# Two modulation vectors held per feature instead of broadcast, with dummy matmuls at launch, the first K in halves, and loads gated by step

## The chip, the cores and the metric

The kernel runs on one core of one Trainium2 chip. The metric is the device time of one execution in microseconds (us); lower is better.

## The reference, cut to what matters

```python
mod = (silu(c) @ w_mod).reshape(1, 6, 1, 640)        # c: (1, 640), w_mod: (640, 3840)
sa, ca, ga, sb, cb, gb = the six vectors of mod

h = layernorm(x) * (1 + ca) + sa                     # x: (2048, 640)
x = x + ga * attention(h, k_cache, v_cache)          # 32 heads of 128, K and V given: 2048 keys
h = layernorm(x) * (1 + cb) + sb
x = x + gb * mixer_and_mlp(h)                        # w1, w2, then w3 (640 x 1728), w4 (1728 x 640)
```

All tensors are bf16. Only `ca` and `sa`, the two vectors of the first line with `h`, are touched by the arithmetic of this change. Everything else in it is about when things are loaded.

## The kernel before

**The build-time schedule.** The program is written as a list of operations on tiles. When the kernel is built, a list scheduler with its own rough cost model puts each engine's operations into a fixed order. On the chip every engine goes through that order and waits on semaphores. Whatever changes a dependence can therefore change the whole order.

```python
    def op(self, eng, fn, dur, reads=(), writes=(), prio=0.0, ..., dep=(), tset=None):
        ...                                   # (cut) read-after-write and write-after-read from tiles
        for d in dep:
            o.deps[d] = True
```

**The stream.** There are 4 chunks (`ch`) of 512 query rows and 32 heads (`h`), so 128 "steps" of some 10 us each. A step loads one head's K (transposed by the DMA), its part of wq and its V, makes Q with five matmuls, and then has eight rounds of two score matmuls, one exp of 128x1024 on ScalarE and eight PV matmuls. The mixer and MLP of chunk `ch` are worked off inside the steps of chunk `ch+1`. All DMA is issued by one engine, SP, in one order.

```python
    def step(ch, h):
        s = ch * H + h
        ...                                   # (cut)
        dma("SP", lambda e: e.dma_start_transpose(k.ap.unsqueeze(1), A_k_cache[0, h]), 560, (), (k,), lp, dur=2600)
        dma("SP", ... w ...)                  # wq of this head, 160 KB
        dma("SP", ... v ...)                  # V of this head, 512 KB
        for kk in range(KT):                  # Q, L462
            P.op("PE", lambda e, kk=kk: e.matmul(m.ap, w[:, kk, :], hT_t[ch % 2][:, kk, :], ...),
                 MM(QC), (w,) + tuple(hT[ch % 2]), (m,), s - 2.0 + 0.17 * kk, accum=True, ...)
        ...                                   # (cut) copy of Q, L465; scores L474, exp L477, PV L487
```

**The modulation vectors.** Each of the six vectors is made on all 128 partitions at once: `s_bc` holds silu(c) repeated 128 times, so ten 128x320 matmuls leave the vector in every row.

```python
    def mod_part(p, stage, prio, dep=()):
        ...                                   # (cut) one load of 800 KB of w_mod
        for hf in range(2):
            ...
                for k in range(KT):           # L340
                    ins = e.matmul(m[:, 0:HD], s_bc[:, k, :], wv[:, k, sl], start=(k == 0), stop=(k == KT - 1))
            ...                               # (cut) ScalarE (L344) or VectorE (L347) copies it out
    mod_part(CA, 0, -98.9)
    mod_part(SA, 1, -98.5)
```

**The first normalisation.** Four row tiles of 128x640 per chunk, each with two VectorE passes that take the vectors as second inputs, then a transposition: by TensorE and a ScalarE copy in chunk 0, by the DMA later. The intermediate `w` is one of three fp32 scratch tiles.

```python
    tmp = ring("tmp", 3, [128, D], F32)

    def get_tmp():
        n_tmp[0] += 1
        return tmp[n_tmp[0] % 3]

    def modulated(src, src_t, mvt, rst, pc, pb, dst, dst_t, prio):
        w = get_tmp()
        P.op("DVE", ... scalar_tensor_tensor(out=w.ap, in0=src, scalar=mvt[:, 0:1], in1=mod_t[pc][:], ...)   # L388
        P.op("DVE", ... scalar_tensor_tensor(out=dst, in0=w.ap, scalar=rst.ap, in1=mod_t[pb][:], ...)        # L391

    def ln1(ch, i, prio):
        j = ch * 4 + i
        x = first_x[j] if j < 4 else load_x(j, prio - 3)
        mvt, rst = ln(x.ap, (x,), prio)
        h = hA[j % 3]
        modulated(x.ap, x, mvt, rst, CA, SA, h.ap, h, prio)
        ...                                   # (cut) transposition into hT
```

**The other loads.** `load_w4` loads all of w4 three times, once per chunk whose MLP is interleaved. `tail_front` loads w1 and w2 once more for the tail, after the stream, into buffers that have come free; nothing but those buffers holds the ten loads back.

```python
    def load_w4(pr):
        for wt, f0, f1 in ((WA, 0, 5), (WA2, 5, 10), (WA3, 10, NF - 1)):
            dma("SP", ... w4 rows f0*128 to f1*128 ...)
        dma("SP", ... the last 64 rows ..., tuple(WA3), pr + 3.5)

        # in tail_front, L751
        for src, dst in ((B_w1, w1p), (B_w2, w2p)):
            for kk in range(KT):
                dma("SP", ..., 160, (), (dst[kk][1],), base - 3)
```

## Time and profile before

| | before |
|---|---|
| time, median of 3 runs | 1452.18 us (1451.65 to 1453.45) |
| span of the profiled run | 1449.9 us |
| first exp of the stream starts | 26.19 us |
| start of the first exp to start of the last | 1321.85 us |
| from the start of the last exp to the end | 101.83 us |

The page of the profile of before, the engines' busy time, the moved bytes, and the shares of the chain that ended last:

```profile
PE 1400.2 (97%) x13129; PEld 934.4 (64%) x13129; DVE 561.3 (39%) x1325; ACT 1099.1 (76%) x1291; POOL 62.3 (4%) x50
...
DMA packets 745769, 228.37 MB, mean 158 GB/s; under 512 B 708320, under 2 KB 744992, under 8 KB 745632
...
PE 90%; ACT 3%; DMA 2%; issue 2%; POOL 1%; DVE 1%; SPq 0%; POOLq 0%
```

TensorE (PE) is busy for 97% of the span and makes up 90% of the chain. So in the stream, work taken from VectorE is worth nothing by itself; what can be won is time in which TensorE has no work or runs at half clock. Only at launch does VectorE stand in the chain.

The launch, from the chain of waits of before (start in us, length in us, what it was):

```profile
1.81 5.01 DMA f_WA<-in_w_mod_dram
...
6.87 2.86 PE f_M L340 x10
...
10.22 0.88 DVE f_tmp L388
...
13.74 1.58 DVE f_hA L391 x2
...
21.99 3.73 PE f_M L462 x9
25.73 0.45 PE f_S L474 x2
26.19 1.03 ACT f_PT L477
```

One load of w_mod, the matmuls of the broadcast, a copy on ScalarE, and then from 10.2 to 20.5 us mostly VectorE work, with passes of 0.88 us, before Q can start at 21.99 us. The nine Q matmuls take 0.41 us each; in the stream two of them take 0.43 us together. The windows view of before (stretch, its length, busy time of PE, PEld, DVE, ACT and POOL with counts, granted TensorE clock, DMA share, GB/s) shows why:

```profile
15.00:20.00 5.00, 1.46 (x11) 0.90 (x10) 4.31 (x9) 2.59 (x7) 0.00 (x0) 0.51 1.14 230
20.00:25.00 5.00, 3.72 (x13) 1.53 (x14) 1.09 (x2) 0.69 (x1) 0.00 (x0) 0.50 0.73 229
```

The granted clock is half. The Trainium skill ("TensorE: Matmul & The Clock Gate", Part 1, "What's actually happening") says that the clock is half until TensorE has been busy for a window of about 3.4 us; this trace agrees as far as the halving goes.

The stream loses time in a few places. In the timeline of the DMA queue (SP) of before, an entry's length is the time that its issue held the queue:

```profile
104.69 1.63 SPq L751 DMA_DIRECT2D f_s_bc<-in_B_w_dram  x1
106.37 2.56 SPq L457 DMA_TRANSPOSE f_KTs<-in_A_k_cache_dram  x1
...
934.63 4.44 SPq L751 DMA_DIRECT2D f_mod<-in_B_w_dram  x3
939.11 2.76 SPq L457 DMA_TRANSPOSE f_KTs<-in_A_k_cache_dram  x1
```

The timeline of ScalarE in the same stretches (in brackets: how long it sat idle before the group, and what released it):

```profile
109.16 6.52 ACT L477 ACTIVATE f_PT<-f_S 128x1024 bf16<-128x1024 f32 x7 [3.01 <-PE f_S L474]
...
946.39 7.73 ACT L477 ACTIVATE f_PT<-f_S 128x1024 bf16<-128x1024 f32 x8 [4.04 <-PE f_S L474]
```

Both times a load of tail weights stands in the queue ahead of a K, and after it exp has no scores for 3 to 4 us. At the second the K landed at 945.47 us and its first scores ran at 945.71. What such a shortage costs TensorE stands in its timeline:

```profile
947.47 0.61 PE L474 MATMUL f_S<-f_QT,f_KTs 128*128 128x512 bf16 x2 [0.68 <-ACT f_PT L477]
948.38 0.60 PE L474 MATMUL f_S<-f_QT,f_KTs 128*128 128x512 bf16 x2 [0.31 <-ACT f_PT L477]
```

With its PV matmuls used up, TensorE makes one pair of scores per exp: a pair every 0.91 us. The view shows a gap of 0.31 us.

A second measure is used in this document, called **lost TensorE time**: the elapsed time of a stretch less the work issued in it, where each matmul counts as its columns at 2.4 GHz plus 2.5 ns. It is an estimate. The two constants are those of the Trainium skill ("TensorE: Matmul & The Clock Gate", "Wait — 56ns, not 53.3ns?"), and this trace agrees nearly: most 512-column matmuls of the stream start 215 ns after the one before and most 129-column ones 56 ns, but some of the latter take 60 and the last one before a pair of scores 70, so eight take 0.46 us in the chain and not 0.45. Counting goes by the weight loads, since some matmul records are missing from some traces.

A caution on the zero of this measure. A recount from the two constants alone comes out higher than the tables below, by some 1.85% of the work in every stretch. With that share taken off, the recount meets every cell within 0.5 us. So the tables' zero is the pace of a stretch that nothing disturbs. Differences between kernels hold to about half a microsecond; a level depends on where the zero is put.

### The profile page before, as it was taken

The numbers are of one execution on the slowest core, as the hardware profiler recorded it, in microseconds if no ns is written. First come the engines' busy times: TensorE is split into PE (matmuls) and PEld (weight loads), VectorE is DVE, ScalarE is ACT, GpSimd is POOL, SyncE is SP. The second block draws the span as 40 slices with busy tenths as digits, with TensorE's granted clock in tenths as the row PEclk, the third lists the DMA queues.
The fourth block names the chain that finished last, engine by engine and source line by source line (L and its number), as shares of the span: only waits on it lengthen the run. The fifth ranks groups of instructions, "written<-read, shape, count | busy, mean of one in ns | idle before, by whom it ended". The sixth has DMA issues, their size and how long they took to land.

```text
span 1449.9 us, 30338 instructions
## 1 busy us (share of the span) xinstructions
PE 1400.2 (97%) x13129; PEld 934.4 (64%) x13129; DVE 561.3 (39%) x1325; ACT 1099.1 (76%) x1291; POOL 62.3 (4%) x50
## 2 busy tenths in 40 slices
PE   5999999999999999999999999999999999999987
PEld 3565666676666666666666666666666656666654
DVE  5332222334742226222844224422464322233662
ACT  4868888887888685788888785678888869887441
POOL 1000000000000000000000000000002100002450
PEclk8999999999999999999999999999999999999999
DMA  7997899999989577998989755999897959886000
GB/s 187 206 221 140 159 173 180 176 202 191 181 160 189 114 144 160 203 176 169 181 172 178 153 115 116 213 199 169 165 177 167 178 99 159 166 167 143 26 6 24
DMA packets 745769, 228.37 MB, mean 158 GB/s; under 512 B 708320, under 2 KB 744992, under 8 KB 745632
## 3 DMA queue, kind: packets, MB, share of 16 engines
q1 hardware_dynamic: 745632, 226.39, 79.1%
q8 instruction: 105, 1.72, 0.5%
q14 instruction: 32, 0.26, 0.1%
HBM read 134.61 MB, written 2.62 MB: 95 GB/s over the span
## 4 chain that ended last, share of the span: by engine, by line
PE 90%; ACT 3%; DMA 2%; issue 2%; POOL 1%; DVE 1%; SPq 0%; POOLq 0%
PE f_O L487 31%; PE f_S L474 29%; PE f_M L462 9%; PE f_M L522 9%; PE f_M L686 3%; ACT f_PT L477 2%; PE f_M L709 2%; PE f_S L903 1%; DMA f_KTs<-in_A_k_cache_dram 1%; PE f_M L887 1%; PE f_M L646 1%; PE f_M L665 1%; PE f_S L860 1%; PE f_M L340 1%; ACT f_us L847 0%
## 5 line engine op out<-in xcount | busy, mean ns | idle before, releaser
L477 ACT ACTIVATE f_PT<-f_S 128x1024 bf16<-128x1024 f32 x1024 | 999.2, 1024 | 224.3 <-PE f_O L487 110.0
L487 PEld LDWEIGHTS f_O<-f_V,f_PT 128*128 128x128 bf16 x8192 | 547.8, 98 | 226.2 <-DVE f_On L498 21.7
L487 PE MATMUL f_O<-f_V,f_PT 128*128 128x129 bf16 x8192 | 641.2, 220 | 1.5 <-DVE f_On L498 0.9
L474 PE MATMUL f_S<-f_QT,f_KTs 128*128 128x512 bf16 x2048 | 602.2, 379 | 16.3 <-ACT f_PT L477 13.3
L465 DVE CAST f_QT<-f_M 128x512 bf16<-128x512 f32 x128 | 88.4, 691 | 476.0 <-PE f_M L462 475.9
L462 PE MATMUL f_M<-f_hT,f_wq 128*128 128x512 bf16 x640 | 226.0, 381 | 0.8 <-ACT f_hT L411 0.8
L474 PEld LDWEIGHTS f_S<-f_QT,f_KTs 128*128 128x128 bf16 x2048 | 165.1, 97 | 82.5 <-ACT f_PT L477 41.0
L522 PE MATMUL f_M<-f_wo,f_OT 128*128 128x320 bf16 x992 | 173.3, 299 | 0.2
L530 DVE TENSOR_TENSOR f_yacc<-f_M,f_yacc 128x320 f32<-128x320 f32 x216 | 105.7, 489 | 146.9 <-PE f_M L522 146.4
L522 PEld LDWEIGHTS f_M<-f_wo,f_OT 128*128 128x128 bf16 x992 | 89.9, 97 | 56.2 <-DVE f_yacc L530 6.0
L498 DVE TENSOR_TENSOR f_On<-f_O,f_rl 128x256 bf16<-128x256 f32 x256 | 107.9, 421 | 6.6
L496 DVE RECIPROCAL f_rl<-f_O 128x2 f32<-128x2 f32 x256 | 43.3, 169 | 159.2 <-PE f_O L487 154.4
L462 PEld LDWEIGHTS f_M<-f_hT,f_wq 128*128 128x128 bf16 x640 | 62.1, 97 | 45.4 <-issue 1.9
L686 PE MATMUL f_M<-f_nT,f_WB 128*128 128x512 bf16 (+3 forms) x210 | 44.1, 362 | 0.0
L690 ACT ACTIVATE f_gT<-f_M 128x512 bf16<-128x512 f32 (+3 forms) x42 | 23.6, 561 | 26.6 <-PE f_M L686 26.6
L709 PE MATMUL f_M<-f_WA,f_gT 128*128 128x320 bf16 x196 | 37.0, 299 | 0.0
L573 POOL COPY f_us<-f_us 128x660 bf16<-128x660 bf16 x3 | 2.2, 736 | 770.2 <-PE f_M L665 770.2
L686 PEld LDWEIGHTS f_M<-f_nT,f_WB 128*128 128x128 bf16 (+1 forms) x210 | 19.6, 98 | 19.6 <-ACT f_gT L690 2.2
L891 ACT ACTIVATE f_gT<-f_M 128x384 bf16<-128x384 f32 (+4 forms) x22 | 11.2, 510 | 18.7 <-PE f_M L887 18.7
L709 PEld LDWEIGHTS f_M<-f_WA,f_gT 128*128 128x128 bf16 x196 | 17.9, 97 | 10.1 <-issue 2.7
L650 ACT ACTIVATE f_us<-f_M 32x512 bf16<-32x512 f32 (+3 forms) x27 | 16.0, 594 | 9.4 <-PE f_M L646 9.0
L903 PE MATMUL f_S<-f_WA,f_gT 128*128 128x320 bf16 (+1 forms) x140 | 21.2, 300 | 0.6 <-ACT f_gT L891 0.6
(126 smaller groups left out, 572.1 us busy)
## 6 DMA issues: line engine op xcount, KB each, us to landing
f_V<-in_A_v_cache_dram SPq DMA_DIRECT2D x128, 512.0 KB, 5.1
f_wq<-in_A_wq_dram SPq DMA_DIRECT2D x128, 160.0 KB, 2.9
f_wo<-in_A_wo_dram SPq DMA_DIRECT2D x32, 640.0 KB, 5.1
f_xin<-in_A_x_dram SPq DMA_DIRECT2D x32, 160.0 KB, 3.5
f_WA<-in_B_w_dram SPq DMA_DIRECT2D x30, 160.0 KB, 3.5
f_WA<-in_B_w_dram SPq DMA_DIRECT2D x6, 800.0 KB, 6.4
out_dram<-f_ob SPq DMA_DIRECT2D x16, 160.0 KB, 1.8
f_WA<-in_w_mod_dram SPq DMA_DIRECT2D x3, 800.0 KB, 5.0
```

Of the source, the lines that this page charges most:

```text
L462: P.op("PE", lambda e, kk=kk: e.matmul(m.ap, w[:, kk, :], hT_t[ch % 2][:, kk, :], start=(kk == 0), stop=(kk == KT - 1)), MM(QC), (w,) + tu ...
L465: P.op("DVE", lambda e: e.tensor_copy(q.ap, m.ap), dve(QC, True), (m,), (q,), s - 4)
L474: ins = e.matmul(sp[:, r * QC:(r + 1) * QC], k[:, kt * 128:(kt + 1) * 128], q.ap, start=True, stop=True)
L477: last_exp[s, j] = P.op("ACT", lambda e, sp=sp, pt=pt: e.activation(pt.ap.rearrange("p k q -> p (k q)"), sp.ap, ACT.Exp, scale=SCALE), 104 ...
L487: ins = e.matmul(o[b][:, u * 129:u * 129 + 129], pt[:, r, qt * 128:(qt + 1) * 128], v[:, kt, 0:129], start=(kt == 0 and u == 0), stop=(kt ...
L496: P.op("DVE", lambda e, ov=ov, i0=i0: e.reciprocal(rl_t[:, i0:i0 + 2].unsqueeze(2), ov[:, 0:258].rearrange("p (u d) -> p u d", u=2)[:, :, ...
L498: P.op("DVE", lambda e, ov=ov, i0=i0, b=b: e.tensor_tensor(out=On_t[gs][:, 2 * b:2 * b + 2, hh, :], in0=ov[:, 0:258].rearrange("p (u d) -> ...
L522: ins = e.matmul(m[:, 0:HD], OT_t[gs][:, qt, hh, :], w[:, hh, sl], start=(hh == 0), stop=(hh == HG - 1))
L530: P.op("DVE", lambda e, m=m, qt=qt, sl=sl: e.tensor_tensor(out=y_t[:, qt, sl], in0=m[:, 0:HD], in1=y_t[:, qt, sl], op=ALU.add), dve(HD, Tr ...
L686: ins = e.matmul(m[0:fs[f], 0:n], w3v[:, kk, f * 128:f * 128 + fs[f]], nT_t[:, kk, r0:r1], start=(kk == 0), stop=(kk == KT - 1))
L709: ins = e.matmul(m[:, 0:HD], gT_t[0:fs[f], f, i * 128:(i + 1) * 128], w4v[0:fs[f], f, sl], start=(f == 0), stop=(f == NF - 1))
L903: ins = e.matmul(m[:, hf * 512:hf * 512 + HD], gT_t[0:fs[f], f, i * 128:(i + 1) * 128], w4v[0:fs[f], f, hf * HD:(hf + 1) * HD], start=(f = ...
```

## The change

The intent as the diff shows it, in five parts.

1. **Per feature.** `ca` and `sa` are no longer broadcast. 50 one-column matmuls leave them as columns, one value per partition (`hm`). The normalisation becomes one VectorE pass without them; after the transposition, where features lie on partitions, five scales of 128x512 apply them. The fp32 scratch tile is not needed any more. The launch gets a new order with it: the x rows are loaded before w_mod, the normalisation goes earlier, and the copy into `s_bc` goes later.
2. **Dummy matmuls.** 144 matmuls of 128x128 at launch, on the identity matrix, to raise the clock.
3. **First K in halves**, so that the first scores need only the first half.
4. **Gates.** The x rows of chunks 1 to 3, and the ten tail weights, may be issued only after the first exp of a given step. The last part of w4 (560 KB) gets loaded once instead of three times.
5. **Own buffer for four tail weights**, as the fp32 vectors whose space they used are gone.

```diff
     def op(self, ...):
-        for d in dep:
-            o.deps[d] = True
+        o.late = dep                    # resolved in schedule(), so that a gate may name a later operation
...
+    for i in range(36):
+        m = Tile(pool="M")
+        def warm(e, m=m):
+            for r in range(4):
+                ins = e.matmul(m[:, r * 128:(r + 1) * 128], ident_t[:], ident_t[:], start=True, stop=True)
+            return ins
+        P.op("PE", warm, 4 * 56, (ident,), (m,), -10)
...
+    for kk in range(KT):
+        def mm_mod(e, kk=kk):
+            for n in range(2 * KT):
+                ins = e.matmul(m_mod[:, n:n + 1], wmv[:, kk, n * 128:(n + 1) * 128], c_f[:, kk:kk + 1], ...)
+            return ins
+        P.op("PE", mm_mod, 2 * KT * 60, (WA[kk], c_f), (m_mod,), -98, accum=True)
...
-    mod_part(CA, 0, -98.9)
-    mod_part(SA, 1, -98.5)
...
     def ln1(ch, i, prio):
-        x = first_x[j] if j < 4 else load_x(j, prio - 3)
+        x = first_x[j] if j < 4 else load_x(j, prio - 3, (lambda: last_exp[ch * H - 22 + 2 * i, 0],))
...
-        modulated(x.ap, x, mvt, rst, CA, SA, h.ap, h, prio)
+        P.op("DVE", lambda e: e.tensor_scalar(out=h.ap, in0=x.ap, scalar1=mvt[:, 0:1], scalar2=rst.ap,
+             op0=ALU.subtract, op1=ALU.mult), 400, (x, mvt, rst), (h,), prio)
...
+    def scale_h(ch, prio):
+        for k in range(KT):
+            v = hT_t[ch % 2][:, k, :]
+            ...                         # k == 2 of chunk 0 on ScalarE
+            P.op("DVE", ... tensor_scalar(out=v, in0=v, scalar1=hm[:, KT + k:KT + k + 1], scalar2=hm[:, k:k + 1],
+                 op0=ALU.mult, op1=ALU.add), 340, tuple(hN[ch % 2]) + (hm,), (hT[ch % 2][k],), prio)
...
     def step(ch, h):
-        dma("SP", lambda e: e.dma_start_transpose(k.ap.unsqueeze(1), A_k_cache[0, h]), 560, (), (k,), lp, dur=2600)
+        for i, (r0, r1) in enumerate(((0, SK // 2), (SK // 2, SK)) if s == 0 else ((0, SK),)):
+            dma("SP", lambda e, r0=r0, r1=r1: e.dma_start_transpose(k[:, r0:r1].unsqueeze(1), ...), ...)
...
-                 MM(QC), (w,) + tuple(hT[ch % 2]), (m,), s - 2.0 + 0.17 * kk, accum=True,
+                 MM(QC), (w, hT[ch % 2][kk]), (m,), s - 2.0 + 0.17 * kk, accum=True,
...
+            dma("SP", ... w4v[:, 10:NF - 1, :] ..., tuple(WA3), base - 16, (last_exp[base - 16, 0],))
+            dma("SP", ... w4v[0:FL, NF - 1, :] ..., tuple(WA3), base - 15, (last_exp[base - 15, 0],))
...
-        for wt, f0, f1 in ((WA, 0, 5), (WA2, 5, 10), (WA3, 10, NF - 1)):
+        for wt, f0, f1 in ((WA, 0, 5), (WA2, 5, 10)):
...
-                dma("SP", ..., 160, (), (dst[kk][1],), base - 3)
+                sl = base - 19 + (n * KT + kk) // 2
+                dma("SP", ..., 160, (), (dst[kk][1],), base - 3, (last_exp[sl, 0],))
```

More of the change, by code (lines that the diff above doesn't have):

```diff
@@ L85, in schedule @@
             o.order = {d() if callable(d) else d for d in o.order}
+            for d in o.late:
+                o.deps[d() if callable(d) else d] = True
             pre = set(o.deps) | o.order
@@ L276, in fast_path @@
     mod = [[T(None), T(None)] for _ in range(6)]
-    mod_t = [sb("mod%d" % i, [128, D], F32) for i in range(6)]
+    mod_t = [None, None] + [sb("mod%d" % i, [128, D], F32) for i in range(2, 6)]
+    hm = T(sb("hm", [128, 2 * KT], F32)[:])
+    wt_t = sb("wt", [128, 4 * D], BF16)
     rl_t = sb("rl", [128, 4 * NC * H], F32)
@@ L302, in back_to_exp @@
         return (o,)
-    c_sb, c_e, c_f = small("c_sb", KT, BF16), small("c_e", KT), small("c_f", KT)
+    c_sb, c_e, c_f = small("c_sb", KT, BF16), small("c_e", KT), small("c_f", KT, BF16)
     s_bc = T(sb("s_bc", [128, KT, 128], BF16)[:])
@@ L313, in fast_path, with load_x @@
     n_x = [0]
-    def load_x(j, prio):
+    def load_x(j, prio, dep=()):
         t = xin[n_x[0] % 4]
         n_x[0] += 1
-        dma("SP", lambda e: e.dma_start(t.ap, x2d[j * 128:(j + 1) * 128, :]), 160, (), (t,), prio)
+        dma("SP", lambda e: e.dma_start(t.ap, x2d[j * 128:(j + 1) * 128, :]), 160, (), (t,), prio, dep)
         return t
-    first_x = [load_x(j, -99 + 0.4 * j) for j in range(4)]
+    first_x = [load_x(j, -99.8 + 0.1 * j) for j in range(4)]
+    wmv = WA_t[:, 0:KT * 2 * D].rearrange("p (k n) -> p k n", k=KT)
+    for kk in range(KT):
+        dma("SP", lambda e, kk=kk: e.dma_start(wmv[:, kk, :], w_mod[kk * 128:(kk + 1) * 128, 0:2 * D]), 320, (), (WA[kk],), -99 + 0.1 * kk)
+    for i in range(36):
[5 more added lines that the diff above has]
+        P.op("PE", warm, 4 * 56, (ident,), (m,), -10)
     P.op("ACT", lambda e: e.activation(c_e.ap, c_sb.ap, ACT.Exp, scale=-1.0), 300, (c_sb,), (c_e,), -90)
@@ L326, in fast_path @@
     P.op("DVE", lambda e: e.tensor_mul(out=c_f.ap, in0=c_e.ap, in1=c_sb.ap), 100, (c_e, c_sb), (c_f,), -90)
-    P.op("DVE", lambda e: e.tensor_copy(s_bc.ap, c_f.ap.unsqueeze(2).to_broadcast([128, KT, 128])), 700, (c_f,), (s_bc,), -90)
+    P.op("DVE", lambda e: e.tensor_copy(s_bc.ap, c_f.ap.unsqueeze(2).to_broadcast([128, KT, 128])), 700, (c_f,), (s_bc,), 0)
+    m_mod = Tile(pool="O1")
+    for kk in range(KT):
+        def mm_mod(e, kk=kk):
+            for n in range(2 * KT):
+                ins = e.matmul(m_mod[:, n:n + 1], wmv[:, kk, n * 128:(n + 1) * 128], c_f[:, kk:kk + 1], start=(kk == 0 and n == 0),
+                               stop=(kk == KT - 1), skip_group_check=True)
+            return ins
+        P.op("PE", mm_mod, 2 * KT * 60, (WA[kk], c_f), (m_mod,), -98, accum=True)
+    P.op("DVE", lambda e: e.tensor_copy(hm[:, 0:KT], m_mod[:, 0:KT]), 170, (m_mod,), (hm,), -98)
+    P.op("DVE", lambda e: e.tensor_scalar(out=hm[:, KT:2 * KT], in0=m_mod[:, KT:2 * KT], scalar1=1.0, scalar2=None, op0=ALU.add),
+         170, (m_mod,), (hm,), -98)
     def mod_part(p, stage, prio, dep=()):
@@ L376, in fast_path @@
     hT_t = [sb("hT%d" % i, [128, KT, QC], BF16) for i in range(2)]
-    hT = [[T(None) for _ in range(4)] for _ in range(2)]
+    hN = [[T(None) for _ in range(4)] for _ in range(2)]
+    hT = [[T(None) for _ in range(KT)] for _ in range(2)]
     hA = ring("hA", 3, [128, D], BF16)
@@ L396, in ln1 @@
         j = ch * 4 + i
-        x = first_x[j] if j < 4 else load_x(j, prio - 3)
+        x = first_x[j] if j < 4 else load_x(j, prio - 3, (lambda: last_exp[ch * H - 22 + 2 * i, 0],))
         mvt, rst = ln(x.ap, (x,), prio)
         h = hA[j % 3]
-        modulated(x.ap, x, mvt, rst, CA, SA, h.ap, h, prio)
-        dst, dt_ = hT_t[ch % 2][:, :, i * 128:(i + 1) * 128], hT[ch % 2][i]
+        P.op("DVE", lambda e: e.tensor_scalar(out=h.ap, in0=x.ap, scalar1=mvt[:, 0:1], scalar2=rst.ap, op0=ALU.subtract, op1=ALU.mult),
+             400, (x, mvt, rst), (h,), prio)
+        dst, dt_ = hT_t[ch % 2][:, :, i * 128:(i + 1) * 128], hN[ch % 2][i]
         if ch == 0:
@@ L413, in ln1 @@
         else:
-            dma("SP", lambda e: e.dma_start_transpose(dst, h.ap), 160, (h,), (dt_,), prio, dur=1250)
+            dma("SP", lambda e: e.dma_start_transpose(dst, h.ap), 160, (h,), (dt_,), prio,
+                tuple(o for t in hT[ch % 2] for o in t.readers[-1:]), dur=1250)
+    def scale_h(ch, prio):
+        for k in range(KT):
+            v = hT_t[ch % 2][:, k, :]
+            if ch == 0 and k == 2:
+                P.op("ACT", lambda e, k=k, v=v: e.activation(v, v, ACT.Identity, scale=hm[:, KT + k:KT + k + 1], bias=hm[:, k:k + 1]),
+                     act(QC), tuple(hN[ch % 2]) + (hm,), (hT[ch % 2][k],), prio)
+                continue
+            P.op("DVE", lambda e, k=k, v=v: e.tensor_scalar(out=v, in0=v, scalar1=hm[:, KT + k:KT + k + 1], scalar2=hm[:, k:k + 1],
+                                                            op0=ALU.mult, op1=ALU.add),
+                 340, tuple(hN[ch % 2]) + (hm,), (hT[ch % 2][k],), prio)
     for i in range(4):
-        ln1(0, i, -80 + i)
+        ln1(0, i, -97 + 0.1 * i)
+    scale_h(0, -96)
     wq = ring("wq", 2, [128, KT, 128], BF16)
     KTs = ring("KTs", 2, [128, SK], BF16)
+    KTh = [[T(None), T(None)] for _ in range(2)]
     V = ring("V", 2, [128, NKT, 130], BF16)
@@ L456, in step @@
         lp = s - 2.5 if s > 1 else -97 + s
-        dma("SP", lambda e: e.dma_start_transpose(k.ap.unsqueeze(1), A_k_cache[0, h]), 560, (), (k,), lp, dur=2600)
+        kh = KTh[s % 2]
+        for i, (r0, r1) in enumerate(((0, SK // 2), (SK // 2, SK)) if s == 0 else ((0, SK),)):
+            dma("SP", lambda e, r0=r0, r1=r1: e.dma_start_transpose(k[:, r0:r1].unsqueeze(1), A_k_cache[0, h, r0:r1, :]), 560 * (r1 - r0) / SK, (),
+                (kh[i],) if s == 0 else tuple(kh), lp, dur=2600 * (r1 - r0) / SK)
         dma("SP", lambda e: e.dma_start(w.ap, A_wq[:, h * 128:(h + 1) * 128].rearrange("(k p) d -> p k d", p=128)), 160, (), (w,), lp - 0.5)
@@ L475, in smm @@
                 return ins
-            last_s[s] = P.op("PE", smm, 2 * MM(QC), (k, q), (sp,), s + j / 8 - 1.0)
+            last_s[s] = P.op("PE", smm, 2 * MM(QC), (kh[j // 4], q), (sp,), s + j / 8 - 1.0)
             last_exp[s, j] = P.op("ACT", lambda e, sp=sp, pt=pt: e.activation(
@@ L559, in load_w123 @@
         if ch == 0:
+            dma("SP", lambda e: e.dma_start(w4v[:, 10:NF - 1, :], B_w4[1280:(NF - 1) * 128, :].rearrange("(f p) n -> p f n", p=128)), 480, (),
+                tuple(WA3), base - 16, (last_exp[base - 16, 0],))
+            dma("SP", lambda e: e.dma_start(w4v[0:FL, NF - 1, :], B_w4[(NF - 1) * 128:FF, :]), 80, (), tuple(WA3), base - 15, (last_exp[base - 15, 0],))
             for kk in range(KT):
@@ L565, in load_w4 @@
     def load_w4(pr):
-        for wt, f0, f1 in ((WA, 0, 5), (WA2, 5, 10), (WA3, 10, NF - 1)):
+        for wt, f0, f1 in ((WA, 0, 5), (WA2, 5, 10)):
             dma("SP", lambda e, f0=f0, f1=f1: e.dma_start(w4v[:, f0:f1, :], B_w4[f0 * 128:f1 * 128, :].rearrange("(f p) n -> p f n", p=128)),
                 160 * (f1 - f0), (), tuple(wt), pr + f0 * 0.3)
-        dma("SP", lambda e: e.dma_start(w4v[0:FL, NF - 1, :], B_w4[(NF - 1) * 128:FF, :]), 80, (), tuple(WA3), pr + 3.5)
     def carry(ch, pr):
@@ L588, in held @@
         fv = [hT_t[0][:].rearrange("p k q -> p (k q)").bitcast(F32)[:, i * D:(i + 1) * D] for i in range(2)]
-        fvt = [like(hT[0]) for _ in range(2)]
+        fvt = [like(hT[0] + hN[0]) for _ in range(2)]
         for t in tl:
@@ L741, in tail_front @@
         carry(ch, base - 2)
-        ca, sa = [mod_t[p][:].bitcast(BF16) for p in (CA, SA)]
-        mca, msa = [[like(mod[p]) for _ in range(2)] for p in (CA, SA)]
+        wt = [(wt_t[:, i * D:(i + 1) * D], T(None)) for i in range(4)]
         on = On_t[0][:].rearrange("p a b c -> p (a b c)")
         ont = [like(On[0]) for _ in range(2)]
-        w1p = [(hA[i].ap, hA[i]) for i in range(3)] + [(ca[:, i * D:(i + 1) * D], mca[i]) for i in range(2)]
-        w2p = [(sa[:, i * D:(i + 1) * D], msa[i]) for i in range(2)] + [(s_bc.ap.rearrange("p k q -> p (k q)"), s_bc)] + \
+        w1p = [(hA[i].ap, hA[i]) for i in range(3)] + wt[0:2]
+        w2p = wt[2:4] + [(s_bc.ap.rearrange("p k q -> p (k q)"), s_bc)] + \
               [(on[:, i * D:(i + 1) * D], ont[i]) for i in range(2)]
-        for src, dst in ((B_w1, w1p), (B_w2, w2p)):
+        for n, (src, dst) in enumerate(((B_w1, w1p), (B_w2, w2p))):
             for kk in range(KT):
-                dma("SP", lambda e, src=src, dst=dst, kk=kk: e.dma_start(dst[kk][0], src[kk * 128:(kk + 1) * 128, :]), 160, (), (dst[kk][1],), base - 3)
+                sl = base - 19 + (n * KT + kk) // 2
+                dma("SP", lambda e, src=src, dst=dst, kk=kk: e.dma_start(dst[kk][0], src[kk * 128:(kk + 1) * 128, :]), 160, (), (dst[kk][1],),
+                    base - 3, (last_exp[sl, 0],))
         return w1p, w2p
@@ L762, in tail @@
         slots = [KTs[0].ap, KTs[1].ap] + [V[i].ap.rearrange("p k d -> p (k d)") for i in range(2)]
-        own = [KTs[0], KTs[1], V[0], V[1]]
+        own = [like(KTh[0]), like(KTh[1]), V[0], V[1]]
         xt = {t0: (x1[t0 % NX], xb[t0 % NX])}
@@ L952, in fast_path @@
                     ln1(ch + 1, i, ch * H + 10 + 2 * i)
+                scale_h(ch + 1, ch * H + 19)
         if ch < NC - 1:
```

## The prediction

> **What bounds the kernel.** TensorE: the page has PE busy 1400.2 of 1449.9 us (ScalarE 1099, VectorE 561), and PE work is 90% of the chain that ended last. Gaps between PE instructions in the trace sum to about 41 us: 14.5 in the first 22 us, about 15 in the attention stream, about 10 in the tail after 1340 us. The change can touch only the first two, so the gain stays below 2%.
>
> **Launch.** The chain of waits before: w_mod load (1.81 to 6.82 us), 128x320 matmuls, ScalarE eviction, then VectorE with eight two-input modulation passes of 0.88 us, BN halves and copies of 0.48 us, PE transposes; Q matmuls at 21.99, first scores at 25.35, first exp at 26.19 us. The Q matmuls ran cold, 0.43 us apart against 0.22 later. The Trainium skill ("TensorE: Matmul & The Clock Gate", Part 1) says the clock is halved until about 3.4 us of activity; the windows view agrees (granted 0.5 from 15 to 25 us).
>
> After: two broadcast vectors become 50 one-column matmuls and two ten-column copies (about 0.2 us each); the eight passes become four one-input bf16 passes (0.61 us from f32 in this trace; estimate 0.4) plus five 128x512 scales (estimate 0.35, one on ScalarE), and Q starts as each scale lands. Summing: last normalised tile near 12.5 us, its transposed copy near 14.5, Q near 15.5, first exp near 18. The 1.6 MB of w_mod should land by 10 to 11 us (before: by 9.6). Halving the first K matters little. The 144 dummy matmuls end near 10 us, about when the first transposes are ready; they may not hold the clock up through the thin stretch to 15 us. Gain: about 8 us, 5 to 9.
>
> **Stream.** The DMA queue issues in order, so a load that waits blocks the next K. Timeline before: a tail weight load into s_bc held it 1.63 us at 104.7, scores ran out, exp sat 3.0 us and PE lost 2.0; three tail loads held it 4.44 us at 934.6, exp sat 4.0 and 2.8 us and PE lost 3.9; at 587.7 a K issue took 6.7 us behind a burst with x and a w4 part, PE lost 1.9; chunk-1 x and w4 loads at 17 to 42 us precede 3 us of PE idle at 60 to 92. The change gates tail loads and x by exp step, and loads the last w4 part once, not three times (1.1 MB less). Gaps at 209 and 1078 us (late K behind transposes, 1.3 and 1.1 us) remain. I expect 6 us back of these 10.8. VectorE work saved later is off the path; the tail is unchanged.
>
> **Predicted: 1438 us**, 1431 to 1446 in 8 of 10. Faster by over 2%: 0.04; within 2%: 0.95; slower: 0.01.
>
> **What would show it.** First exp at 17 to 20 us (timeline); Q matmuls 0.22 us apart; no queue wait of microseconds on tail weight loads, no exp gap of 3 us near 100 and 930 us; PE gaps about 27 us in all; VectorE busy some 15 us lower; 1 MB less moved.
>
> **What would make it wrong.** w_mod landing after 11 us, or dummy matmuls holding back the transposes, loses half the launch gain. A cold clock at Q costs 1 to 2 us. The rescheduled stream could open new late-K gaps of 1 to 3 us that cancel the 6; or more K delays than the PE gaps show could vanish, down to 1431.

## More of the kernel before

A state is known only for repeated runs. Every run told of here was in the fast state, so all comparisons are of fast runs with fast runs.

(Before the first clock record of a trace, which lies at 11.64 us in before, the view reads 1.00 whatever the clock was: ten 320-column matmuls took 2.86 us at 6.87 us, and 1.36 us in the stream.)

## The result, and the profile after

| | before | after |
|---|---|---|
| time, median | 1452.65 us (4 runs) | 1431.85 us (4 runs, 1430.38 to 1433.18) |
| ratio to before, 95% interval | | 0.9857 (0.984 to 0.9874) |
| span of the profiled run | 1449.9 us | 1429.5 us |
| first exp starts | 26.19 us | 19.51 us |
| start of the first exp to start of the last | 1321.85 us | 1308.42 us |
| from the start of the last exp to the end | 101.83 us | 101.61 us |

A ratio is the mean time of one kernel's runs over that of the other's of the same rounds, so it is not quite the ratio of the medians in the table. The kernel is 1.4% faster, which is inside the 2% that counts as the same. The 20.8 us of the medians stand against 14 predicted. In the profiled runs 6.7 us come from the launch, 13.4 from the stream and 0.2 from the tail.

The page of after:

```profile
PE 1387.8 (97%) x13078; PEld 943.8 (66%) x13303; DVE 550.2 (38%) x1328; ACT 1102.9 (77%) x1291; POOL 62.3 (4%) x50
...
DMA packets 744254, 227.28 MB, mean 159 GB/s; under 512 B 708336, under 2 KB 742832, under 8 KB 744112
...
PE 91%; issue 3%; ACT 2%; POOL 1%; DVE 1%; DMA 1%; POOLq 0%; DVEq 0%
```

1.09 MB less are moved and VectorE is busy 11.1 us less. The PE count must not be compared with that of before: there are 13303 weight loads and only 13078 matmuls, so 225 matmul records are missing.

The launch, from the chain of after:

```profile
1.53 10.11 PE f_M L333 x128
11.63 0.23 PE f_O L346 x10
11.86 0.32 PE f_M L432 x5
...
12.20 0.70 ACT f_hT L435
...
16.25 0.75 DVE f_hT L448 x2
...
17.04 1.05 PE f_M L503 x4
...
18.87 0.62 PE f_S L515 x2
...
19.51 1.95 ACT f_PT L518 x2
```

The load of w_mod and the VectorE passes are gone from it. In their place stand 128 dummy matmuls, up to 11.63 us. The Q matmuls are now 0.26 us apart or less, so the clock is up. In VectorE's timeline of after, the first two normalised tiles were done long before the dummies ended:

```profile
8.19 0.79 DVE L423 TENSOR_SCALAR f_hA<-f_xin,f_mv,f_rs 128x640 bf16<-128x640 bf16 x2
```

Their transpositions wait from 8.98 us to the end of the dummies: TensorE works off its order, and the dummies stand first in it.

In the stream, the DMA queue of after at the place of the second loss:

```profile
932.97 0.37 SPq L500 DMA_DIRECT2D f_V<-in_A_v_cache_dram  x1
933.40 5.76 SPq L497 DMA_TRANSPOSE f_KTs<-in_A_k_cache_dram  x1
```

ScalarE there:

```profile
924.67 6.33 ACT L518 ACTIVATE f_PT<-f_S 128x1024 bf16<-128x1024 f32 x6 [0.35 <-PE f_S L515]
931.63 2.85 ACT L518 ACTIVATE f_PT<-f_S 128x1024 bf16<-128x1024 f32 x3 [0.62 <-PE f_O L528]
```

No tail weight stands ahead of the K, and exp waits tenths of a microsecond. (The first place did not come out as clean: a wait of 4.82 us before the exp at 89.56 us remains in after; TensorE had other work in it.)

Where the time came from, by step, as lost TensorE time (the estimate defined above, us). The columns are stretches of steps; "start" is when the first exp starts. Losses below zero are the error of the estimate.

| kernel | start | 0–10 | 10–52 | 52–60 | 60–84 | 84–92 | 92–127 | sum of 0–127 |
|---|---|---|---|---|---|---|---|---|
| before | 26.19 | 9.7 | 1.0 | 3.1 | 1.1 | 5.4 | 2.5 | 22.8 |
| after | 19.51 | 4.2 | 0.0 | 0.3 | 1.5 | 0.7 | 2.0 | 8.7 |

The sum falls by 14.1 us; the stream itself is 13.4 us shorter, so differences are good to within a microsecond here. The same count is used for the experiments below. The gain has three sites: steps 0 to 10 (5.5 us), steps 52 to 60 (2.8) and steps 84 to 92 (4.7).

The sites at 52 and 84 lie where chunk `ch+1` of the normalised rows is made. In before's VectorE timeline, the first pass of the normalisation (L388) comes just after the output stage (L713 to L716), again and again:

```profile
547.67 0.82 DVE L716 TENSOR_TENSOR f_ob<-f_tmp,f_x 128x640 bf16<-128x640 f32 x1
...
548.75 0.88 DVE L388 SCALAR_TENSOR_TENSOR f_tmp<-f_xin,f_mv,f_mod 128x640 f32<-128x640 bf16 x1
```

Its four transposed tiles enter the DMA queue at steps 52, 52, 53 and 54 in before, and at 43, 45, 47 and 49 in after. In chunk 3 the steps are 83 to 86 in before, and 75 to 81 in after. Chunk 1's enter at steps 1 to 2 in before and, with x gated, at 11 to 17 in after; that bears on the first site. So there was a second candidate for the stream's gain, which the prediction did not have: the normalisation was held back by the three scratch tiles that it shared with the output stage, and bunched with that stage's loads, stores and matmuls.

### The profile page after: what moved, and what is told of

It is laid out like the page before. It is cut to its first block, busy times and chain, and to the rows that moved or that the text cites. A ratio compares the mean times of both kernels' runs of the same rounds, so it can differ in the third digit from the quotient of the medians.

```text
span 1429.5 us, 30451 instructions
## 1 busy us (share of the span) xinstructions
PE 1387.8 (97%) x13078; PEld 943.8 (66%) x13303; DVE 550.2 (38%) x1328; ACT 1102.9 (77%) x1291; POOL 62.3 (4%) x50
## 4 chain that ended last, share of the span: by engine, by line
PE 91%; issue 3%; ACT 2%; POOL 1%; DVE 1%; DMA 1%; POOLq 0%; DVEq 0%
PE f_O L528 32%; PE f_S L515 29%; PE f_M L563 9%; PE f_M L503 9%; PE f_M L729 3%; PE f_M L752 2%; PE f_S L947 1%; PE f_M L931 1%; DMA f_KTs<-in_A_k_cache_dram 1%; PE f_M L689 1%; PE f_M L708 1%; ACT f_PT L518 1%; PE f_M L333 1%; PE f_S L904 1%; ACT f_us L891 0%
## 5 line engine op out<-in xcount | busy, mean ns | idle before, releaser
L515 PE MATMUL f_S<-f_QT,f_KTs 128*128 128x512 bf16 x1885 | 567.4, 379 | 16.2 <-ACT f_PT L518 4.7
L503 PE MATMUL f_M<-f_hT,f_wq 128*128 128x512 bf16 x585 | 207.9, 378 | 1.9 <-DVE f_hT L448 1.4
L733 ACT ACTIVATE f_gT<-f_M 128x512 bf16<-128x512 f32 (+3 forms) x42 | 23.4, 561 | 21.2 <-PE f_M L729 21.2
L947 PE MATMUL f_S<-f_WA,f_gT 128*128 128x320 bf16 (+1 forms) x140 | 21.2, 300 | 0.6 <-ACT f_gT L935 0.6
```

What stands on the lines that cost most here:

```text
L515: ins = e.matmul(sp[:, r * QC:(r + 1) * QC], k[:, kt * 128:(kt + 1) * 128], q.ap, start=True, stop=True)
L947: ins = e.matmul(m[:, hf * 512:hf * 512 + HD], gT_t[0:fs[f], f, i * 128:(i + 1) * 128], w4v[0:fs[f], f, hf * HD:(hf + 1) * HD], start=(f = ...
```

## The experiments

The leading theory was that the gates give the stream's gain and the per-feature form the launch's. The rivals: the scratch tiles (just told), the dummies, the halves of K, and that any new order of the stream would do. Twelve kernels were run, in three jobs, each job on one chip with before beside it. All gave correct results.

### Do the gates alone give the stream's gain?

Kernel before with all three gates of part 4 and nothing else:

```diff
-        x = first_x[j] if j < 4 else load_x(j, prio - 3)
+        x = first_x[j] if j < 4 else load_x(j, prio - 3, (lambda: last_exp[ch * H - 22 + 2 * i, 0],))
...
+            dma("SP", ... w4v[:, 10:NF - 1, :] ..., base - 16, (last_exp[base - 16, 0],))    # once
+            dma("SP", ... w4v[0:FL, NF - 1, :] ..., base - 15, (last_exp[base - 15, 0],))    # once
...
-        for wt, f0, f1 in ((WA, 0, 5), (WA2, 5, 10), (WA3, 10, NF - 1)):
+        for wt, f0, f1 in ((WA, 0, 5), (WA2, 5, 10)):
...
-                dma("SP", ..., (dst[kk][1],), base - 3)
+                sl = base - 19 + (n * KT + kk) // 2
+                dma("SP", ..., (dst[kk][1],), base - 3, (last_exp[sl, 0],))
```

> The kernel before, with all three gates of the change (tail weight loads by exp step, last w4 part loaded once and by step, chunk x loads by step) and nothing of the launch. Theory 1, the in-order DMA queue: the late K loads near steps 4, 8, 56 and 87 vanish and it gains 12 to 14 us by itself (about 1439 us), first exp still near 26.2 us. Rival: the launch rework reshuffled the list schedule and the VectorE work, the gates alone give the 6 us that were forecast (about 1446 us).

Measured: 1444.03 us, ratio 0.9941 (0.9925 to 0.9957). First exp at 26.51 us; the stream took 1314.19 us, 7.7 less than before. The result lies between the two expectations: the gates account for somewhat more than half of the stream's 13.4 us, and not for the rest.

### Each gate by itself

The three gates singly, each with the diff lines of its own from above.

> The kernel before, with the tail weight loads alone gated. Theory 1: the losses at step 8 (3.0 us) and steps 87 to 89 (5.2 us) go, others stay: 6 to 8 us faster, about 1445 us. Rival (reshuffle): 2 us or less.

> The kernel before, with the last part of w4 loaded once, by step. Theory 1: the losses at steps 56 to 57 (2.75 us) go and part of step 4: 2 to 4 us faster, about 1449 us; 1.1 MB less moved. Rival: within 1 us of before.

> The kernel before, with the x loads of chunks 1 to 3 gated by step. Theory 1: losses at steps 4 to 6 (4.2 us) go: 3 to 5 us faster, about 1448 us. Rival: within 1 us of before.

| kernel | time, us | ratio (95%) | stream, us |
|---|---|---|---|
| tail weights gated | 1448.14 | 0.997 (0.9954 to 0.9987) | 1319.79 |
| w4's last part loaded once | 1446.41 | 0.9957 (0.9943 to 0.9972) | 1315.62 |
| x gated | 1449.73 | 0.9983 (0.9967 to 0.9999) | 1320.29 |

The same estimate of lost TensorE time for all four:

| kernel | start | 0–10 | 10–52 | 52–60 | 60–84 | 84–92 | 92–127 | sum of 0–127 |
|---|---|---|---|---|---|---|---|---|
| tail weights gated | 26.32 | 9.0 | 2.2 | 2.9 | 2.0 | 2.9 | 1.8 | 20.8 |
| w4 part once | 26.64 | 7.6 | −0.2 | 2.4 | 1.2 | 4.9 | 1.0 | 16.9 |
| x gated | 26.91 | 5.4 | 2.0 | 3.6 | 1.7 | 6.9 | 1.8 | 21.4 |
| all three | 26.51 | 5.4 | 1.9 | 1.9 | 2.2 | 1.9 | 1.7 | 15.0 |

Two gates cure something near where they act: the x gate takes 4.3 us from steps 0 to 10, the tail gate 2.5 us from steps 84 to 92. But the x gate alone makes steps 84 to 92 worse by 1.5 us, so it ends 2.4 us faster by the medians and not 3 to 5; and the tail gate, which left the loss at step 8 standing, 4.0 us faster and not 6 to 8. The gate on w4 does the most, 5.8 us against 2 to 4 expected, and mostly elsewhere than expected: by the tables 2.1 us of its gain lie in steps 0 to 10, 1.2 in 10 to 52 and 1.5 after 92, and only 0.7 in steps 52 to 60, where 2.75 were to go. Their stream gains add up to 9.9 us against 7.7 for the three together. The parts do not add. Every gate makes the scheduler order the whole stream anew, which is the likely reason.

The tail gate also refutes a reading of the prediction, that the tail weight loaded into s_bc at 104.7 us caused the wait at 109 us. The DMA queue with that gate alone:

```profile
99.93 0.52 SPq L460 DMA_DIRECT2D f_V<-in_A_v_cache_dram  x1
104.77 2.48 SPq L458 DMA_TRANSPOSE f_KTs<-in_A_k_cache_dram  x1
```

And ScalarE with it:

```profile
108.81 7.44 ACT L478 ACTIVATE f_PT<-f_S 128x1024 bf16<-128x1024 f32 x8 [3.01 <-PE f_S L475]
```

The weight is gone from the queue, the next K is issued at 104.77 in place of 106.37 us, and exp still waits 3.01 us. In before, moreover, the K that step 8 needs had landed at 101.95 us, and its first scores ran only at 108.47 us. They stood behind other matmuls in TensorE's own order, as the chain of before shows:

```profile
107.32 1.37 PE f_O L487 x24
108.69 0.45 PE f_S L474 x2
```

The loss of that step (3.1 us by the recount) is down to 0.3 us in the kernels that gate x without the rest of the change, and to the same in the one that gates only w4's part, though step 9 then loses 1.4 in place of 0.3. So several new orders cure most of it, and why the scheduler orders step 8 so stays open.

### The scratch tiles: freed in before, taken again in after

Kernel before with all gates, and the first pass of the normalisation written into its own result tile instead of a scratch tile:

```diff
-    def modulated(src, src_t, mvt, rst, pc, pb, dst, dst_t, prio):
-        w = get_tmp()
+    def modulated(src, src_t, mvt, rst, pc, pb, dst, dst_t, prio, w=None):
+        w = w or get_tmp()
...
-        modulated(x.ap, x, mvt, rst, CA, SA, h.ap, h, prio)
+        modulated(x.ap, x, mvt, rst, CA, SA, h.ap, h, prio, h)
```

The intermediate is bf16 then.

> The three gates on the kernel before, as in gates_all, and the first modulation pass of chunks' entry written into its own output tile instead of the shared scratch ring (the sum is then rounded to bf16 between the passes). Theory S, the scratch ring held the next chunk's entry back until the feed-forward of the chunk before was written out (steps 51 to 53), and its x loads and transposes then crowd out K: the losses at steps 56 to 57 and 88 to 89 go, 4 to 5 us faster than gates_all (about 1440 us, ratio near 0.991). Rival R, the cheaper bf16 VectorE passes of the change are what freed the stream: no more than 1 us faster than gates_all (1444 us).

And the reverse: kernel after, with its one pass claiming a scratch tile that it does not use, so that it waits for the output stage as before did:

```diff
-             400, (x, mvt, rst), (h,), prio)
+             400, (x, mvt, rst), (h, get_tmp()), prio)
```

> The changed kernel with the scratch ring's ordering put back: the normalising pass also claims a tile of the shared ring, which it doesn't use. Arithmetic and VectorE time as in the changed kernel. Theory S: the entry moves back to steps 51 to 53, K late at steps 56 to 57 and 88 to 89, 3 to 5 us slower than the changed kernel (ratio near 0.988). Rival R: within 1 us of it (ratio near 0.985).

| kernel | time, us | ratio (95%) | stream, us | 0–10 | 10–52 | 52–60 | 60–84 | 84–92 | 92–127 |
|---|---|---|---|---|---|---|---|---|---|
| before, gates, scratch freed | 1440.08 | 0.9925 (0.991 to 0.994) | 1309.27 | 5.4 | 0.8 | 0.8 | 1.8 | 0.3 | 1.3 |
| after, scratch taken | 1434.7 | 0.989 (0.9873 to 0.9908) | 1312.91 | 4.3 | 0.3 | 2.4 | 1.3 | 2.4 | 2.0 |

Freeing the scratch moves the four transpositions from steps 52 to 54 back to 43 to 49 (75 to 81 in chunk 3), and takes the stream from 1314.19 to 1309.27 us, 0.9 us from that of after. Taking it again in after moves them to steps 51 to 54 and lengthens the stream by 4.5 us, at just the two sites. The rival of the cheaper passes is out: in before with the scratch freed, the two passes take 883 and 882 ns, as in before (878 and 879). The second pair is also clear in the measured times: its interval does not touch that of after run again in another job (0.9839 to 0.9866), and it meets that of the result only at the edge (0.984 to 0.9874). The first pair is not quite (0.991 to 0.994 beside 0.9925 to 0.9957, from different chips); there the verdict rests on the profiles.

ScalarE's timeline shows it near step 56. All gates, scratch shared:

```profile
594.67 4.69 ACT L478 ACTIVATE f_PT<-f_S 128x1024 bf16<-128x1024 f32 x5 [2.33 <-PE f_S L475]
...
604.92 5.70 ACT L478 ACTIVATE f_PT<-f_S 128x1024 bf16<-128x1024 f32 x6 [2.32 <-PE f_S L475]
```

All gates, scratch freed:

```profile
596.43 2.85 ACT L478 ACTIVATE f_PT<-f_S 128x1024 bf16<-128x1024 f32 x3 [0.63 <-PE f_O L488]
599.55 7.95 ACT L478 ACTIVATE f_PT<-f_S 128x1024 bf16<-128x1024 f32 x8 [0.27 <-PE f_O L488]
```

And after, scratch taken:

```profile
584.95 8.01 ACT L518 ACTIVATE f_PT<-f_S 128x1024 bf16<-128x1024 f32 x8 [1.96 <-PE f_S L515]
595.27 5.70 ACT L518 ACTIVATE f_PT<-f_S 128x1024 bf16<-128x1024 f32 x6 [2.32 <-PE f_S L515]
```

Two waits of 2.3 us for scores become waits of 0.3 to 0.6 us, and come back as 2.0 and 2.3 us when the scratch is taken again. The chain from the scratch tile to the wait is partly open: at step 57 with all gates, K had landed at 600.48 and Q was there by 596.24 us, but the first scores ran at 604.24. So here too they stood behind other matmuls in the planned order, and the bunched work is what the order had to place. Which matmul should have been elsewhere was not tested.

### The per-feature form alone

Kernel after without gates, dummies and halves:

```diff
-    for i in range(36):
+    for i in range(0):
...
-        x = first_x[j] if j < 4 else load_x(j, prio - 3, (lambda: last_exp[ch * H - 22 + 2 * i, 0],))
+        x = first_x[j] if j < 4 else load_x(j, prio - 3)
...
-        for i, (r0, r1) in enumerate(((0, SK // 2), (SK // 2, SK)) if s == 0 else ((0, SK),)):
+        for i, (r0, r1) in enumerate(((0, SK),)):
...                                       # w4 and the tail weights loaded as in before
-        wt = [(wt_t[:, i * D:(i + 1) * D], T(None)) for i in range(4)]
+        wt = [(wt_t[:, i * D:(i + 1) * D], like([hA[2]])) for i in range(4)]
```

The last line lets the four tail weights wait for hA, as without gates nothing else would hold them.

> The change without its gates, dummy matmuls and K halves: only the two vectors held per feature, their loads in row blocks and the scales on transposed rows (tail weight loads tied to the normalised-row ring, as the buffers of before were). If the parts add, the gain is the total less the 8 us of gates_all: 11 to 13 us (about 1440 us), of it 6.5 to 8 before the first exp and the rest at steps 42 to 62 and 75 to 92 from the freed scratch ring. Rival: without the gates the x loads still crowd the queue and it gains only the 7 us of the launch (about 1446 us).

Measured: 1443.5 us, ratio 0.9948 (0.9932 to 0.9963). First exp at 18.45 us, which is 7.7 us sooner than in before. The stream took 1321.18 us, only 0.7 us less. So the whole launch gain comes with the per-feature form, and the stream gain from it is nothing, although its scratch is free. This kernel keeps the new order of the launch (x first, normalisation earlier); how much of the 7.7 us is the form and how much that order was not separated. By stretches:

| kernel | start | 0–10 | 10–52 | 52–60 | 60–84 | 84–92 | 92–127 | sum of 0–127 |
|---|---|---|---|---|---|---|---|---|
| per feature only | 18.45 | 11.1 | 1.3 | 0.3 | 7.0 | 0.3 | 1.2 | 21.2 |

At steps 52 to 60 and 84 to 92 it is as good as after; it gives that back at steps 75 to 77. The DMA queue there:

```profile
782.40 1.21 SPq L438 DMA_TRANSPOSE f_hT<-f_hA  x1
...
784.28 2.08 SPq L321 DMA_DIRECT2D f_xin<-in_A_x_dram  x1
786.41 2.57 SPq L497 DMA_TRANSPOSE f_KTs<-in_A_k_cache_dram  x1
```

And ScalarE:

```profile
783.50 7.53 ACT L518 ACTIVATE f_PT<-f_S 128x1024 bf16<-128x1024 f32 x8 [4.23 <-PE f_S L515]
794.15 6.52 ACT L518 ACTIVATE f_PT<-f_S 128x1024 bf16<-128x1024 f32 x7 [3.12 <-PE f_S L515]
```

With the scratch free but nothing gated, x rows, a transposition and tail weights stand here in the queue ahead of a K. That this crowding is the cause is not shown: the K of step 75 had landed at 779.17 us and that of step 76 at 791.08, their first scores ran only at 782.82 and 793.47, and TensorE worked without a gap until then. As at step 8, the scores stood behind other matmuls. By the recount steps 75 to 77 lose 5.7 us here and 0.5 in after, with the gates. This kernel and the one with gates alone bring 16 us together (8.6 and 7.5, worked out from the ratios), and after brings 21: part 1 and part 4 seem to help each other (the intervals are about 2 us either way).

### The dummies, and the first K in halves

After once more, in the same job as the three that follow:

> The changed kernel again, as the control on this chip for the three beside it: 20 to 21 us faster than before (about 1432 us), first exp near 19.5 us.

After with no dummies (`range(36)` becomes `range(0)`), with half of them (`range(18)`), and with the first K in one piece:

> The changed kernel without the 144 dummy matmuls. Theory A, they hold back the transposes (128 of them end at 11.6 us, the first two normalised tiles are ready at 9.0): first exp comes at 16 to 18 us, but Q and the first scores run cold and the first steps lose 2 to 3 us, so the end is within 1.5 us of the changed kernel. Rival, the clock is what pays: Q and scores cold and first exp no earlier than 19.5 us, end 2 us or more later than the changed kernel.

> The changed kernel with 72 dummy matmuls in place of 144. Theory A: they end near 8.4 us, the clock has risen by 7.4 us and stays up, first exp at 16.5 to 17.5 us, end 2 to 3 us earlier than the changed kernel (about 1429.5 us). Rival: the clock falls again in the thin stretch and the end is the same within 1 us or later.

> The changed kernel with the first K loaded whole. Theory: K lands before Q is ready either way, same within 1 us and first exp within 0.3 us. Rival: halves matter, first exp over 1 us later.

| kernel | time, us | ratio (95%) | Q starts, us | first exp, us |
|---|---|---|---|---|
| after, again | 1431.88 | 0.9852 (0.9839 to 0.9866) | 15.66 | 18.45 |
| no dummies | 1431.1 | 0.9842 (0.9829 to 0.9856) | 14.21 | 18.38 |
| 72 dummies | 1429.7 | 0.9831 (0.9818 to 0.9845) | 13.68 | 17.86 |
| first K whole | 1431.27 | 0.9846 (0.9832 to 0.9859) | 15.58 | 18.44 |

All intervals overlap. Neither the dummies nor the halves do anything that these runs can show. The chain without dummies tells why the dummies don't:

```profile
8.67 0.73 PE f_M L432 x5
...
9.42 1.29 ACT f_hT L435 x2
...
14.21 2.33 PE f_M L503 x5
...
17.30 1.05 PE f_S L515 x2
...
18.38 1.03 ACT f_PT L518
```

The transposition starts at 8.67 us, not at 11.86, and Q at 14.21. But Q and the first scores run cold: 2.33 us for five Q matmuls where after again took 1.38, and 1.05 us for the first scores where it took 0.62. What the dummies win in clock they cost in waiting. Part of the waiting goes through ScalarE: the copies of the first two transposed tiles (L435) stand in its order before two small operations (L394, L395) that the other two tiles need. The last normalised tile is done at 14.66 us in after and at 11.88 without dummies.

Of the expectations, that for the whole K came true. Without dummies the end was as expected, but the first exp came at 18.38 us and not at 16 to 18. With 72 the theory failed and the rival was right: by the clock records of the trace the clock rose at 5.99 us and fell to half again from 12.82 to 23.06 us, so five Q matmuls ran cold in the chain:

```profile
13.68 2.33 PE f_M L503 x5
```

The four executions with 128 dummies in front also show how tightly the dummies hold the launch:

| kernel | dummies end, us | first exp, us | difference |
|---|---|---|---|
| after | 11.63 | 19.51 | 7.88 |
| after, again | 10.57 | 18.45 | 7.88 |
| first K whole | 10.49 | 18.44 | 7.95 |
| after, scratch taken | 10.30 | 18.17 | 7.87 |

The same 128 matmuls took 8.8 to 10.1 us, and the first exp came 7.9 us after their end each time. The Trainium skill ("TensorE: Matmul & The Clock Gate", Part 1, "What's actually happening") says that the activity window runs freely, so that the moment at which the clock rises varies from run to run. These four agree: their clock records have the rise at 7.41, 5.19, 5.03 and 4.61 us, and 55, 34, 33 and 29 of the dummies ran at the cold pace of 0.107 us. The spread of 2.8 us is wider than the 500 ns either way that the section gives.

### A version that should have beaten both

The dummies were cut to fit before the first transpositions (68), with 44 more between the later ones, in TensorE's score banks, and a VectorE copy was moved out of the way:

```diff
-    for i in range(36):
-        m = Tile(pool="M")
+    def dummies(n, after=()):                 # 17 at launch, 6 and 5 after two transpositions
+        for i in range(n):
+            m = Tile(pool="S")
...
-    P.op("DVE", ... tensor_copy(s_bc.ap, ...) ..., 0)
+    P.op("DVE", ... tensor_copy(s_bc.ap, ...) ..., 0, after=(lambda: hA_op[3],))
```

> The changed kernel with 68 dummy matmuls before the first transposes and 44 in the gaps after them, in a bank pair that nothing waits for, and the broadcast copy of the vector moved behind the launch's VectorE chain. Theory A: the transposes start near 8 us and the clock stays up through Q; first exp at 15.5 to 17 us, 2 to 3.5 us faster than the changed kernel (ratio near 0.983). Rival: the clock falls again or the dummies stand in the way, ratio 0.985 or above.

Measured: 1430.16 us, ratio 0.9858 (0.9837 to 0.9879), the same as after. Q ran warm (five in 1.38 us) from 14.68 us, and the first exp came at 17.46 us, 1.0 us sooner than in after run again but later than the 15.5 to 17 expected. The ratio is the rival's, but not for the rival's reason: the trace's clock is full from 5.69 us through the whole stream. The stream took 1308.18 us, and steps 4 to 10 lost 4.1 us in place of 3.0. The microsecond was gone at step 7 (its first exp at 88.54 us, against 88.50 in after run again). The loss is in step 6; its K had landed at 66.78 us, 6.7 us before the first scores, so the cause is open.

## Why the prediction was right or wrong

**The bound, right.** TensorE bounds the kernel, and the gain stayed below 2%. The range held the result by 0.85 us only (1431.85 against 1431): its width saved it, while the sum was 6.6 us short. The prediction had named "more K delays than the PE gaps show" as the way down to 1431, so the size was allowed for; the cause told below was not in it.

**The launch, nearly right in sum, and wrong in one step.** 8 us were predicted, and 6.7 measured in the profiled run of after, 7.7 in its second one. The kernel with the per-feature form and the new order at launch, without dummies, has all 7.7. The estimates of the new operations held: 0.4 us for a normalising pass (two in 0.79 us), 0.35 us for a scale (the four on VectorE at launch took 1.38 us); the one scale on ScalarE took 0.81. The step that failed is "the 144 dummy matmuls end near 10 us, about when the first transposes are ready". The first 128 ended between 10.3 and 11.6 us and the other 16 by 12.8 to 14.2, while the first tiles were ready by 9. So the dummies set the launch, which was named as a risk; the last normalised tile came at 14.66 us and not at 12.5.

**The halves of K, right.** "Halving the first K matters little": first exp at 18.44 and 18.45 us without and with it.

**The stream, right in direction and half the size.** 6 us were predicted, "of these 10.8", and 13.4 came. The term can be taken apart with the table of lost time:

- *The places were measured too small.* The 10.8 us were gaps as the timeline shows them. By elapsed time less work, the same places (steps 4–10, 52–60 and 84–92) lost 7.6 + 3.1 + 5.4 = 16.1 us. A pair of score matmuls is recorded as 0.60 us when it waits, and takes 0.43 when it does not. A gap shown as 0.31 us was a loss of 0.48.
- *How much of it came back.* 6 of 10.8 is 56%. After still loses 4.0 us in those places, so 12.1 of 16.1 came back, 75%. This share depends on the zero of the estimate: the recount from the two constants alone has 12.0 of 20.2, 60%. That a larger share came back than assumed is therefore not shown.
- *The cause that was missed.* Gates alone give 7.7 us, which is near the 6. The freed scratch gives 4.9 more on top of them. Together 12.6 of the 13.4 us are explained, and the reverse experiment, 4.5 us, agrees. Without the gates the freed scratch gave the stream only 0.7 us in sum. The prediction counted the removed fp32 tile as VectorE time "off the path" and did not ask what that tile was waiting for.
- *"Gaps at 209 and 1078 us remain", wrong.* Steps 18 to 24 lost 2.1 us in before and −0.2 in after, and the step at 1078 us (step 101) 1.4 and 0.1 by the recount.

**The cause of a single gap, wrong.** "A tail weight load into s_bc held it 1.63 us at 104.7, scores ran out": with the load gone the wait of 3.01 us stayed. What came just before a gap in the queue was taken for its cause, without a look at when the K of that step had landed.

**The rest.** 1.1 MB less was predicted and 1.09 came. VectorE was to be 15 us less busy and is 11.1. The tail is unchanged, 0.2 us. "PE gaps about 27 us in all" can't be judged, since records are missing in after.

**What stays open.** At step 8 of before and step 57 with all gates, K and Q were ready and the scores ran later, so the planned order holds them; that the order is also why single gates help or hurt far from where they act is likely but not shown, and which rule of the scheduler does it was not isolated. The rival that any new order of the stream would do had no experiment of its own: no run reordered the stream without meaning. The scratch pair, which moves the same two sites both ways, speaks against it there; step 8, most of whose loss three different gatings cure, does not. The last 0.8 us of the stream's gain have no experiment of their own.

## What to carry to other kernels

When a change removes a temporary buffer, look at who else draws from the same ring: here, with the gates in place, freeing it was worth more than half of what the three deliberate gates were worth, and in the stream that gain came without any VectorE time saved. Measure a stall as elapsed time less work and not as the recorded gap, and before a load is blamed for it, check whether the data it delays was the last thing missing. Dummy work that raises a clock stands in the same order as the real work and can hold it back; here none of the numbers tried, 0, 72 or 144, nor a version fitted into the gaps, ended measurably apart.

## What the Trainium skill lacked or had wrong

- "TensorE: Matmul & The Clock Gate", Part 1: right about the free-running window, but it puts the spread of the rise at 500 ns either way, and here it came 3.1 to 5.9 us after the first dummy. These runs also give the price in a launch: the same 128 dummies took 8.77 to 10.11 us, and the first exp moved with them from 18.17 to 19.51 us. The page does not say that warming matmuls delay the work behind them; with 144, 72 and 0 of them the ratios to before were 0.9852, 0.9831 and 0.9842, which the noise does not tell apart.
- The same page, on reading the clock: the granted clock of the windows view was 1.00 in all stretches of the run without dummies, from 5 to 25 us, while five Q matmuls of 512 columns took 2.33 us, against 1.38 us warm. The first clock record of that trace is the rise at 21.01 us, and the view takes what comes before a first record as full. The page warns that clock records can be unreliable; no page says that a trace need not tell of the cold stretch before its first one.
- "Perfetto Trace Analysis", "Tensor Engine Instruction (MATMUL, LD_WEIGHTS)": it says that a matmul's recorded end is an estimate, and these traces agree. The page warns against the matmuls' busy share, but lacks what follows for gaps: gaps between matmuls understate idle time. Two 512-column matmuls stand as 0.60 us after a wait and take 0.43 in a busy stretch, so a gap of 0.31 us was a loss of 0.48. Nor does it say that records can be missing: 224 to 226 matmul records were, in each of five of these traces.
- "VectorE: DVE Perf Modes", "The perf-mode tier table": it gives 693 ns for a bf16 tensor_scalar of 2048 elements. In after, 640 columns took 444 ns on average (16 passes) and 512 columns 406 ns (19 passes). With the fixed part of some 158 cycles that the page itself gives, 640 columns would take 331 ns (an estimate): a quarter less than the record, and near the 340 to 360 ns from one pass's start to the next's. A row for a short size, and whether a record or a start-to-start time is meant, would help.
- No page treats the order that a build-time scheduler fixes. In before, the score matmuls of step 8 ran 6.5 us after their K had landed (101.95 to 108.47 us), with no wait in the trace that named the cause.
